# Sliding-window attention and an MLP on one core: another order for batch 3's exponentials, and one crossbar transposition ahead of six loads

## The chip, the core and the metric

The kernel runs on one core of a Trainium2 chip. A core has five engines, each with an instruction queue of its own that is worked off in order: TensorE (matrix products and transpositions, PE in the profile, with PEld for its weight loads), VectorE (DVE), ScalarE (ACT), GpSimd (POOL) and SyncE (SP), which in this kernel issues nearly all DMAs. They meet only through semaphores: an instruction that needs another engine's result waits at the head of its queue, and everything behind it waits too.

The metric is the device time of one execution in microseconds (us). The kernel before took 301.85 us, the median of three runs from 301.53 to 302.24.

## The reference

Eight batches, eight heads, 576 positions, 64 columns a head. Attention looks back over a window of 64 positions; the result, with heads side by side (512 columns), goes through a layer norm and a two-layer MLP with 2048 hidden units, and is added to itself:

```python
scores = scale * np.matmul(q, k.transpose(0, 1, 3, 2))
mask = (rel >= 0) & (rel < window)            # rel = query position - key position, window = 64
attn = softmax(np.where(mask, scores, -1e9))
x = np.matmul(attn, v)                        # then [batch, seq, heads * 64]
xn = (x - mu) / np.sqrt(var + 1e-06) * g_ln
out = x + np.maximum(xn @ w_ch1, 0.0) @ w_ch2
```

## The kernel before

**Groups and blocks.** The first 512 positions of a batch make a group (groups 0 to 7); the last 64 positions of all batches make group 8, the "tails", two batches to a block. A group has four blocks of 128 rows, written (group, block): (3,2) is the third block of batch 3.

**Attention of a block.** `s_pe` makes the scores on TensorE, the even heads in one PSUM bank and the odd ones in another ("par" 0 and 1, the two halves of a block). `s_exp` takes the exponential of one half on ScalarE (line 359), into the tile `pt`. `s_mask` multiplies both halves by the window's mask on VectorE (L369). `b_pe` multiplies by v on TensorE (L396, tile `xps`); `b_rows` divides by the row sums and takes mean and variance on VectorE (L416 to L429). `z_step` makes the norm's factors on GpSimd (tile `rsz`, L448 to L450) and, from group 3 on, the normalised rows z (L454); for group 2 `z_act` does the rows on ScalarE (L460). `zt_step` transposes z into `zT`, which layer 1 reads: on SyncE by a crossbar DMA (L474), or for the last block of groups 2, 3 and 5 on TensorE into the tile `ztp` (L478) with a copy by ScalarE (L481).

**Where the score tiles live.** PSUM is full, so scores borrow banks. For batch 3: (3,0) and (3,2) use the two "sc" banks, (3,1) the "xps" banks, which `b_pe` of (3,0) uses next, and (3,3) the banks "t0" and "t1", which the transpositions on TensorE use next, the `ztp` of (2,3) first among them.

**The MLP of a group** is a list of units. Group 2 has 30. Units 0 to 15 are layer 1 (`l1_half`, L642): eight matmuls into one of two PSUM buffers ("mm", used in turn), and a relu by ScalarE (L647) that frees the buffer. Units 0 to 7 read the first 256 rows of `zT`, units 8 to 15 the other 256. Units 16 to 29 are layer 2 in seven products (L575), whose results VectorE adds to x (L584, L588), and then SyncE stores. From group 3 on a layer-1 unit reads all 512 rows (L501).

**The order is written out by hand.** While the MLP of group g runs, the attention of batch g+1 is put between its units: `at(i, f, ...)` puts a call behind unit i, in slot i. Each engine gets its instructions in the order in which the calls are made, so a slot says at once where a call stands in the queue of every engine that it uses. The change moves entries of slots of g == 1 (slot 29) and g == 2.

**SyncE's queue in g == 2**, in the order of the slots: stores of the group before; `load_qk` and `load_v` of batch 4 (slots 0 and 3); `load_tail` of tail block 0, six loads, q, k and v of two batches (slot 4, L104 to L106); `zt_step` of (3,0) (slot 8); the two crossbar transpositions of batch 4's q (slot 13, L265); `zt_step` of (3,1) and (3,2) (slots 14 and 18); then copies of v (L201, L203), stores, and the loads of the next batch. `cast_tail` (GpSimd, L115 to L118) reads the tail loads in slot 24.

**GpSimd in g == 2**: the factors and rows z of the blocks, `after_mask` (L362), a one-element copy that reads the last masked tile and so holds GpSimd's casts of batch 4 (L154) until VectorE has finished the masks, the casts of v (L182) and the tails. z has three buffers, so z(3,3) takes the one of z(3,0) once its transposition has read it.

Of the kernel before, what the change touches and what calls it, by code (L numbers as in the profile page):

```python
# [18 lines left out]
def kernel(  # L19
# [927 lines left out]
    for g in range(NGRP):  # L947
# [7 lines left out]
        def at(i, f, *a):  # L955
            slots[min(i, len(slots) - 1)].append((f, a))
# [56 lines left out]
        if g == 1:  # L1013
            at(0, cast_qk, 2, 0, (0,))
            at(0, after_mask, 1, 3)
            at(0, cast_qk, 2, 0, (1,))
            at(0, cast_qk, 2, 1, (0,))
            at(0, alloc_v, 2)
            at(0, alloc_qkT, 2)
            at(1, t_main, 2, 0, 0)  # L1020
            at(1, b_pe, 1, 2, "t")
            at(1, b_pe, 1, 3, "sc")
            at(1, b_rows, 1, 2)
            at(1, z_step, 1, 2)
            at(1, b_rows, 1, 3)
            at(1, z_step, 1, 3)
            at(1, cast_qk, 2, 1, (1,))
            at(2, z_dve, 1, 2)
            at(3, t_main, 2, 1, 0)
            at(4, t_main, 2, 0, 1)  # L1030
            at(4, z_dve, 1, 3)
            for c in (0, 2):
                at(4, cast_v, 2, c, c + 2)
                at(5, part_vB, 2, c)
            at(5, zt_step, 1, 2)
            at(7, zt_step, 1, 3, "dve")
            at(10, t_main, 2, 1, 1)
            for n, i in enumerate((3, 2, 4)):
                at(8, w2_sums, i, 4, 8)
            at(7, s_pe, 2, 0)  # L1040
            at(7, s_pe, 2, 1, False, "xps")
            at(8, s_exp, 2, 0, 0, 1)
            at(9, s_mask, 2, 0)
            at(9, w2_sums, 1, 0, 8)
            at(10, s_exp, 2, 1, 0)
            at(11, s_exp, 2, 1, 1)
            at(12, s_sums, 0, 4, 1, 2)
            at(12, s_mask, 2, 1)
            at(16, s_sums, 4, 8, 1, 2)
            at(20, s_sums, 0, 8, 3)  # L1050
            at(22, s_sums, 0, 8, 4)
            for j in range(4):
                i = (13, 16, 22, 22)[j]
                at(i, b_pe, 2, j, "sc" if j == 3 else "xps")
                if j < 2:
                    at(i, s_mm, 2, j + 2)
                    at(19, s_mask, 2, j + 2)
                i = (13, 17, 25, 25)[j]
                at(i, b_mult, 2, j)
                if j == 3:  # L1060
                    i = 30
                at(i, b_stats, 2, j)
                at(i, z_step, 2, j)
                if j < 3:
                    at((17, 20, 26)[j], z_act, 2, j)
                    at((17, 20, 26)[j], zt_step, 2, j)
            at(6, load_qk, 3, 0)
            at(8, load_qk, 3, 1)
            at(10, load_v, 3, 0, 4)
            at(8, alloc_qkT, 3)  # L1070
            at(8, cast_qk, 3, 0)
            at(14, cast_qk, 3, 1, (0,))
            at(17, cast_qk, 3, 1, (1,))
            at(18, alloc_v, 3)
            at(18, cast_v, 3, 0, 2)
            at(18, cast_v, 3, 2, 4)
            at(21, part_vB, 3, 0, 4)
            at(29, s_pe, 3, 0)
            at(29, s_pe, 3, 1, False, "xps")
            at(29, s_exp, 3, 0, 0, 1)  # L1080
            for i, (x, half) in zip((12, 21, 18, 24), ((0, 0), (1, 0), (0, 1), (1, 1))):
                at(i, t_main, 3, x, half, 0)
        if g == 2:
            at(0, load_qk, 4, 0)
            at(0, load_qk, 4, 1)
            at(0, s_exp, 3, 1, 0)
            at(0, s_mask, 3, 0)
            at(1, s_exp, 3, 1, 1)
            at(2, s_mask, 3, 1)
            at(3, load_v, 4, 0, 4)  # L1090
            at(3, b_pe, 3, 0)
            at(3, s_pe, 3, 2)
            at(3, s_pe, 3, 3, False, "t")
            at(6, zt_step, 2, 3, "act")
            for i, x in enumerate(((2, 0), (2, 1), (3, 0), (3, 1))):
                at(3 + i, s_exp, 3, *x)
            at(4, z_act, 2, 3)
            at(5, s_mask, 3, 2)
            at(5, b_rows, 3, 0)
            at(5, z_step, 3, 0)  # L1100
            at(7, s_mask, 3, 3)
            at(7, alloc_qkT, 4)
            at(7, after_mask, 3, 3)
            at(7, cast_qk, 4, 0)
            at(7, cast_qk, 4, 1)
            for j in range(1, 4):
                at(9, b_pe, 3, j, ("xps", "t", "sc")[j - 1])
                at((9, 10, 12)[j - 1], b_rows, 3, j)
                at((9, 10, 12)[j - 1], z_step, 3, j)
            for j, i in enumerate((8, 14, 18, 25)):  # L1110
                at(i, zt_step, 3, j)
        elif g > 1 and b < B:
            tail = TAILS.get(g)
            at(2, b_pe, b, 0)
            at(2, b_rows, b, 0)
            at(2, z_step, b, 0)
            at(2, s_pe, b, 2)
            at(2, s_exp, b, 2, 0, 1)
            at(3, s_mask, b, 2)
            if tail:  # L1120
                r, i = NGRP - 1, tail[0]
                at(2, s_pe, r, i, False, "t")
                at(4, s_exp, r, i, 0)
                at(5, s_exp, r, i, 1)
                at(5, s_mask, r, i)
                at(7, b_pe, b, 1)
                at(7, b_pe, r, i, "t")
                at(7, s_mm, b, 3)
                at(7, b_rows, b, 1)
                at(7, z_step, b, 1)  # L1130
                at(8, s_mask, b, 3)
                at(8, b_rows, r, i)
                at(9, z_step, r, i)
                at(12, b_pe, b, 2)
                at(12, b_pe, b, 3, "sc")
                at(16, zt_step, r, i)
            else:
                at(2, s_pe, b, 3, False, "t")
                at(4, s_exp, b, 3, 0)
                at(5, s_exp, b, 3, 1)  # L1140
                at(5, s_mask, b, 3)
                at(7, b_pe, b, 1)
                at(7, b_pe, b, 2, "t")
                at(7, b_pe, b, 3, "sc")
                at(7, b_rows, b, 1)
                at(7, z_step, b, 1)
            if g + 2 < B:
                at(5, alloc_qkT, g + 2)
                at(5, after_mask, *((NGRP - 1, tail[0]) if tail else (b, 3)))
                at(5, cast_qk, g + 2, 0)  # L1150
                at(5, cast_qk, g + 2, 1, (0,))
                at(11, cast_qk, g + 2, 1, (1,))
            for j, i in ((2, 12), (3, 19)):
                at(i, b_rows, b, j)
                at(i, z_step, b, j)
            for j in range(4):
                at((2, 14, 18, {3: 25, 5: 25}.get(b, 23))[j], zt_step, b, j)
# [31 lines left out]
                at((15, 15, 20, 22)[i - 1], s_sums, 6, 8, i)  # L1189
        for n, i in enumerate(TAILS.get(g + 1, ())):  # L1190
            if n == 0:
                at(4, load_tail, i)
                at(24 if i < 2 else 18, cast_tail, i)
                at(27 if i < 2 else 22, t_tail, i, 0)
                at(29 if i < 2 else 22, t_tail, i, 1)
            else:
                at(25, load_tail, i)
# [48 lines left out]
```

## Time and profile before

| what | before |
|---|---|
| median of three runs | 301.85 us (301.53 to 302.24) |
| the profiled execution | 301.72 us, clock of TensorE 0.996 |
| its span, first to last instruction | 300.0 us |
| TensorE busy | 290.4 us, 97% |
| VectorE, GpSimd, ScalarE busy | 219.3, 164.9, 154.4 us |
| a relu, L647 | 0.60 us |
| an exponential of a half, L359 | 0.60 us |
| a layer-1 matmul of 256 columns, L642 | 0.27 us, pipelined |

A line of the timeline gives the start and the length in us, the engine, the line of the kernel, the operation, output and inputs, their shapes and how many were merged; brackets at its end hold the time that the engine sat idle before it and who ended that. A line of the waits gives who waited for whom: us in total, times, longest. Instructions of one engine overlap in the pipeline, so that one starts 0.48 us behind the last although each takes 0.60. The DMA issues of SyncE (SPq) give the time of issuing, not of the transfer; how long a transfer takes to land is told by tile, as minimum, median and maximum.

Of the stretch that the change touches: unit 0 of group 2 starts at 87.70 us, the first unit of group 3 at 121.05.

### The profile page before, as it was taken

What the parts mean: (1) busy time and instruction counts of PE and PEld (TensorE: products, weight loads), DVE (VectorE), ACT (ScalarE), POOL (GpSimd) and SP (SyncE); (2) the same over time, 40 slices, a digit from 0 to 9 for tenths busy, and PEclk for the clock granted to TensorE, in tenths of its full rate; (3) what the DMA queues carried; (4) which work ended last, traced back from release to release, by engine and by line L of the source; (5) the groups of instructions that cost most, each with busy time, mean ns of one, the idle gap of its engine ahead of it and who ended that gap; (6) DMA issues with size and microseconds to landing.
All of it is one profiled execution on the core that took longest, in us unless ns stands there. A gap on an engine that the chain in (4) does not pass through costs nothing.

```text
span 300.0 us, 7816 instructions
## 1 busy us (share of the span) xinstructions
PE 290.4 (97%) x3183; PEld 206.2 (69%) x3183; DVE 219.3 (73%) x414; ACT 154.4 (51%) x260; POOL 164.9 (55%) x243
## 2 busy tenths in 40 slices
PE   7889999999998999999999999999999999999993
PEld 3657545888887888547854786469646854788883
DVE  2771398899984794679757866699568785789982
ACT  4576647587348624874177428842574056306500
POOL 4688886765741986289608960788038407024300
PEclk9999999999999999999999999999999999999998
DMA  7999999979968999999299998991729498003014
GB/s 188 260 379 341 385 287 286 237 227 301 181 132 272 265 189 167 252 291 164 51 266 305 188 176 263 298 162 39 219 46 184 69 174 199 20 17 142 1 37 105
DMA packets 113765, 58.22 MB, mean 194 GB/s; under 512 B 83137, under 2 KB 104705, under 8 KB 113730
## 3 DMA queue, kind: packets, MB, share of 16 engines
q1 hardware_dynamic: 113296, 57.34, 79.1%
q8 instruction: 25, 0.41, 0.6%
q10 hardware_dynamic: 434, 0.40, 0.4%
q14 instruction: 10, 0.08, 0.1%
HBM read 38.80 MB, written 9.44 MB: 161 GB/s over the span
## 4 chain that ended last, share of the span: by engine, by line
PE 85%; DMA 4%; SPq 4%; POOL 2%; issue 1%; ACT 1%; DVE 1%; POOLq 0%; ACTq 0%
PE hps L501 26%; PE pA L575 12%; PE hph L642 10%; PE pB L575 9%; PE pC L575 8%; PE xps L396 4%; PE ch L659 4%; PE sc L349 3%; DMA w1s<-in_moe_w_ch_dram 3%; PE lA L698 2%; PE tp L276 2%; SPq L176 2%; DMA zT<-z 1%; SPq L87 1%; PE lC L698 1%
## 5 line engine op out<-in xcount | busy, mean ns | idle before, releaser
L501 PE MATMUL hps<-zT,w1g 128*128 128x512 f16 x352 | 80.2, 379 | 0.0
L505 ACT ACTIVATE hrT<-hps 128x512 f16<-128x512 f32 x88 | 52.8, 600 | 36.8 <-PE hps L501 33.7
L501 PEld LDWEIGHTS <-w1g 128*128 128x128 f16 x352 | 33.1, 98 | 38.0 <-issue 1.8
L575 PEld LDWEIGHTS <-sS 128*128 128x128 f16 x512 | 49.4, 98 | 5.7
L359 ACT ACTIVATE pt<-sc 128x512 f16<-128x512 f32 x72 | 39.7, 601 | 19.6 <-PE sc L349 18.9
L448 POOL TENSOR_SCALAR rsz<-mvg 128x1 f32<-128x1 f32 x32 | 10.5, 328 | 64.3 <-DVE mvg L429 54.6
L575 PEld LDWEIGHTS <-hrT 128*128 128x128 f16 x384 | 36.7, 98 | 6.9 <-ACT hrT L505 0.8
L369 DVE TENSOR_TENSOR pt<-pt,mask 128x1024 f16<-128x1024 f16 x32 | 24.6, 775 | 20.1 <-ACT pt L359 20.1
L642 PE MATMUL hph<-zT,w1g 128*128 128x256 f16 x320 | 38.1, 273 | 0.3 <-ACT hrT L647 0.2
L154 POOL CAST qk<-qk 128x1024 f16<-128x1024 f32 x29 | 33.0, 1157 | 8.2 <-DMA qk<-in_q_dram 6.6
L642 PEld LDWEIGHTS <-w1g 128*128 128x128 f16 x320 | 30.4, 98 | 5.0 <-issue 0.4
L575 PE MATMUL pC<-w2s,sS 128*128 128x256 f16 x256 | 30.9, 273 | 0.0
L575 PE MATMUL pA<-wT,sS 128*128 128x256 f16 x256 | 30.9, 273 | 0.0
L647 ACT ACTIVATE hrT<-hph 128x512 f16<-128x512 f32 x40 | 23.9, 601 | 11.4 <-PE hph L642 11.1
L257 ACT COPY qkT<-tp 128x1024 f16<-128x1024 f16 (+1 forms) x18 | 17.3, 963 | 23.1 <-PE tp L276 22.1
L549 DVE TENSOR_TENSOR sS<-hrT 128x1024 f16<-128x1024 f16 (+2 forms) x41 | 27.3, 665 | 1.8 <-ACT hrT L505 1.8
L420 DVE TENSOR_TENSOR xn<-xps,rcp 128x256 f32<-128x256 f32 (+1 forms) x50 | 25.8, 539 | 1.5 <-DMA out_dram<-xn 0.8
L426 DVE BATCH_NORM_STATS2 stats<-xn 128x6 f32<-128x512 f32 x36 | 25.0, 695 | 1.2
L454 POOL TENSOR_SCALAR z<-xn,rsz 128x512 f16<-128x512 f32 x24 | 22.3, 928 | 5.2 <-DMA zT<-z 2.8
L449 POOL TENSOR_TENSOR rsz<-rsz,mhalf 128x1 f32<-128x1 f32 x32 | 21.0, 658 | 2.7
L182 POOL CAST vA<-v 128x1024 f16<-128x1024 f32 (+1 forms) x18 | 17.1, 964 | 4.2 <-DMA v<-in_v_dram 4.0
L396 PEld LDWEIGHTS <-pt 128*64 128x64 f16 x576 | 11.6, 110 | 9.6 <-issue 5.1
(120 smaller groups left out, 418.8 us busy)
## 6 DMA issues: line engine op xcount, KB each, us to landing
qk<-in_q_dram SPq DMA_DIRECT2D x16, 512.0 KB, 6.1
qk<-in_k_dram SPq DMA_DIRECT2D x16, 512.0 KB, 6.7
out_dram<-xn SPq DMA_DIRECT2D x32, 256.0 KB, 3.1
v<-in_v_dram SPq DMA_DIRECT2D x28, 256.0 KB, 7.1
w2s<-in_moe_w_ch_dram SPq DMA_DIRECT2D x9, 512.0 KB, 8.4
w1s<-in_moe_w_ch_dram SPq DMA_DIRECT2D x4, 512.0 KB, 7.4
tk<-in_k_dram SPq DMA_DIRECT2D x8, 256.0 KB, 4.5
tv<-in_v_dram SPq DMA_DIRECT2D x8, 256.0 KB, 5.1
```

Source lines behind the costliest of these rows:

```text
L154: nc.gpsimd.tensor_copy(out=dst[:, :].rearrange("p (a j) e d -> p a e j d", j=j), in_=t[:, :].rearrange("p (a e j d) -> p a e j d", e=2, j ...
L359: nc.scalar.activation(out=o, in_=i, func=AF.Exp, bias=0.0, scale=scale)
L369: nc.vector.tensor_tensor(out=ptv, in0=ptv, in1=mb, op=ALU.mult)
L396: nc.tensor.matmul(out=tiles[h // n][64 * r:64 * r + 64, h % n, :D + 1], lhsT=pt[:, par, hp, r, :], rhs=rhs, start=True, stop=True)
L420: nc.vector.tensor_tensor(out=xn[:, n * i:n * i + n], in0=xps[:, :, 0:D], in1=rcp_b, op=ALU.mult)
L426: nc.vector.bn_stats(out=stats, in_=xv)
L501: nc.tensor.matmul(out=hps, lhsT=w1g[:, kc, 128 * hc:128 * (hc + 1)], rhs=zT[g][:, kc, :], start=(kc == 0), stop=(kc == NKC - 1),)
L505: nc.scalar.activation(out=hrT[:, hc, :], in_=hps, func=AF.Relu, bias=0.0, scale=1.0)
L549: nc.vector.tensor_tensor(out=o, in0=x, in1=y, op=op)
L575: nc.tensor.matmul(out=o, lhsT=a[:, c, 128 * p:128 * p + 128], rhs=wv[:, c, :], start=(first and (p == 0 or split_c) and c == 0), stop=(c ...
L642: nc.tensor.matmul(out=hps[:, e], lhsT=w1g[:, kc, 128 * hc:128 * (hc + 1)], rhs=zT[g][:, kc, 256 * half:256 * half + 256], start=(kc == 0) ...
L647: nc.scalar.activation(out=hrT[:, 2 * i:2 * i + 2, 256 * half:256 * half + 256], in_=hps, func=AF.Relu, bias=0.0, scale=1.0)
```

## The change

Three things. The second half of (3,0)'s exponentials goes from slot 29 of g == 1 to slot 0 of g == 2, and the halves of (3,1) from slots 0 and 1 to slots 1 and 2. The exponentials of (3,3) come ahead of those of (3,2), and the masks likewise; `after_mask` follows the mask that is now the last. And in g == 2 the six tail loads go from slot 4 to slot 9, behind the crossbar transposition of z(3,0) in slot 8; in other groups they stay in slot 4.

```diff
         if g == 1:
...
-            at(29, s_exp, 3, 0, 0, 1)
+            at(29, s_exp, 3, 0, 0)
...
         if g == 2:
             at(0, load_qk, 4, 0)
             at(0, load_qk, 4, 1)
-            at(0, s_exp, 3, 1, 0)
+            at(0, s_exp, 3, 0, 1)
             at(0, s_mask, 3, 0)
-            at(1, s_exp, 3, 1, 1)
+            at(1, s_exp, 3, 1, 0)
+            at(2, s_exp, 3, 1, 1)
             at(2, s_mask, 3, 1)
             at(3, load_v, 4, 0, 4)
             at(3, b_pe, 3, 0)
             at(3, s_pe, 3, 2)
             at(3, s_pe, 3, 3, False, "t")
             at(6, zt_step, 2, 3, "act")
-            for i, x in enumerate(((2, 0), (2, 1), (3, 0), (3, 1))):
+            for i, x in enumerate(((3, 0), (3, 1), (2, 0), (2, 1))):
                 at(3 + i, s_exp, 3, *x)
             at(4, z_act, 2, 3)
-            at(5, s_mask, 3, 2)
+            at(5, s_mask, 3, 3)
             at(5, b_rows, 3, 0)
             at(5, z_step, 3, 0)
-            at(7, s_mask, 3, 3)
+            at(7, s_mask, 3, 2)
             at(7, alloc_qkT, 4)
-            at(7, after_mask, 3, 3)
+            at(7, after_mask, 3, 2)
...
         for n, i in enumerate(TAILS.get(g + 1, ())):
             if n == 0:
-                at(4, load_tail, i)
+                at(9 if g == 2 else 4, load_tail, i)
```

## The prediction

> **What bounds the kernel now.** I read, in this order, the page's busy times, TensorE's waits, TensorE's timeline around the change, then ScalarE, GpSimd and SyncE in the same stretch.
>
> ```profile
> PE 290.4 (97%) x3183; PEld 206.2 (69%) x3183; DVE 219.3 (73%) x414; ACT 154.4 (51%) x260; POOL 164.9 (55%) x243
> ```
>
> TensorE is the bound, so the change can only win what TensorE idles. All of its waits from 85 to 121 us, the stretch that the change touches (the same view from 121 us to the end is empty: afterwards TensorE never waits, so a gain or a loss at 121 us goes through to the end one to one):
>
> ```profile
> PE ztp L478 <- ACT pt L359: 1.1, 1, 1.1
> PE ztp L478 <- POOL z L454: 0.3, 1, 0.3
> PE hph L642 <- ACT hrT L647: 0.2, 1, 0.2
> ```
>
> Their places in TensorE's timeline; the last column is idle time and who ended it:
>
> ```profile
> 89.85 2.01 PE L642 MATMUL hph<-zT,w1g 128*128 128x256 f16 x16 [0.23 <-ACT hrT L647]
> ...
> 96.64 0.38 PE L478 MATMUL ztp<-ident,z 128*128 128x128 f16 x4 [1.10 <-ACT pt L359]
> ...
> 115.94 0.40 PE L478 MATMUL ztp<-ident,z 128*128 128x128 f16 x4 [0.25 <-POOL z L454]
> ```
>
> Matmuls are pipelined, so I count in start times. Eight matmuls of a unit take 0.87 us (1.75 for 16, as 83.53 to 85.28 shows). Unit 2 could have started at 87.70 + 1.75 = 89.45 and started at 89.85: 0.40 lost. The ztp at 96.64 could have started at 92.74 + 24 x 0.109 = 95.36: 1.28 lost. The one at 115.94 could have at 113.78 + 1.75 = 115.53: 0.41 lost.
>
> ScalarE, where the first two waits end (L359 exponentials, L647 relus, L460 and L481 the normalised rows z(2,3) and the copy of their transpose):
>
> ```profile
> 93.83 0.60 ACT L647 ACTIVATE hrT<-hph 128x512 f16<-128x512 f32 x1 [0.62 <-PE hph L642]
> 94.32 0.59 ACT L359 ACTIVATE pt<-sc 128x512 f16<-128x512 f32 x1
> 94.80 0.81 ACT L460 ACTIVATE z<-xn,rsz 128x512 f16<-128x512 f32 x1
> 95.51 0.59 ACT L647 ACTIVATE hrT<-hph 128x512 f16<-128x512 f32 x1
> 95.98 0.60 ACT L359 ACTIVATE pt<-sc 128x512 f16<-128x512 f32 x1
> 96.46 0.61 ACT L647 ACTIVATE hrT<-hph 128x512 f16<-128x512 f32 x1
> 97.06 0.59 ACT L481 COPY zT<-ztp 128x512 f16<-128x512 f16 x1
> 97.54 0.60 ACT L359 ACTIVATE pt<-sc 128x512 f16<-128x512 f32 x1
> 98.03 0.60 ACT L647 ACTIVATE hrT<-hph 128x512 f16<-128x512 f32 x1
> ```
>
> The reader is to see that no row from 94.32 to 98.03 has an idle time behind it: ScalarE works without a pause while TensorE waits 1.10. One starts every 0.48 us (0.71 behind z). GpSimd and SyncE, where the third wait comes from:
>
> ```profile
> 115.12 0.77 POOL L454 TENSOR_SCALAR z<-xn,rsz 128x512 f16<-128x512 f32 x1 [2.79 <-DMA zT<-z]
> ```
> ```profile
> 94.79 8.68 SPq L176 DMA_DIRECT2D v<-in_v_dram  x4
> 103.51 1.03 SPq L104 DMA_DIRECT2D tq<-in_q_dram  x1
> 104.59 0.64 SPq L105 DMA_DIRECT2D tk<-in_k_dram  x1
> 105.27 1.09 SPq L106 DMA_DIRECT2D tv<-in_v_dram  x1
> 106.41 1.45 SPq L104 DMA_DIRECT2D tq<-in_q_dram  x1
> 107.91 1.64 SPq L105 DMA_DIRECT2D tk<-in_k_dram  x1
> 109.58 1.01 SPq L106 DMA_DIRECT2D tv<-in_v_dram  x1
> 110.71 1.69 SPq L474 DMA_TRANSPOSE zT<-z  x1
> ```
>
> z(3,3) has three buffers to rotate through and takes the one of z(3,0); z(3,0) is written by 99.88, but its transposition is issued only at 110.71, behind v and the six tail loads.
>
> **Part 1: the exponentials.** Eight remain, at the same 0.48 us; TensorE's order does not change. Worked forward with these rows, a relu starting 0.22 behind the last matmul start slot of its unit (unit ends 101.42, relu 101.64), and TensorE 0.05 behind a release (relu ended 89.80, unit 2 started 89.85). exp(3,0,0) 88.25; relu 0, which waits for unit 0 (87.70 + 0.87 + 0.22), 88.79; exp(3,0,1) 89.27; relu 1 89.75; exp(3,1,0) 90.23; relu 2 90.71; exp(3,1,1) 91.19, done 91.79. Unit 2 then starts at 89.45, so the 0.40 goes. But b_pe(3,0) writes into the "xps" banks that held the scores (3,1), and those are free only at 91.79: it starts at 91.85, where it started at 91.79 before. The stall has moved and become 0.06 longer.
>
> From there: scores until 92.80; unit 4; relu 4 at 92.80 + 0.87 + 0.22 = 93.89 (93.83 before). exp(3,3,0) fits before it, in ScalarE's pause of 0.62. Behind relu 4 the same list runs as in the rows above, only with (3,3,1) first and (3,2,0), (3,2,1) later: z 94.86, relu 5 95.57, exp 96.04, relu 6 96.52, copy 97.00, exp 97.48, relu 7 97.96, done 98.56. The wait of the ztp does go: the (3,3) scores sat in the banks it needs, their exponentials now end at 94.98, and it starts behind z at 95.73. But unit 9 reuses the PSUM buffer of unit 7 and needs relu 7: 98.61, against 98.03 + 0.60 + 0.05 = 98.68 before. Units 7 and 8 wait for relus 5 and 6 and for the copy (97.59), which unit 8, the first on rows 256 to 511, reads. Of 1.28 us TensorE keeps 0.07. The release of "xps" I take for the whole tile; if it goes by bank, half of b_pe(3,0)'s 32 matmuls (0.38 us) run before the wait and the gain is 0.2 more.
>
> What else moves is covered. DVE masks (3,3) first and (3,2) last, at about 98.2 to 98.8; b_pe(3,2) comes at 100. The mask of (3,0) ends at 90.6 instead of 90.2, needed at 91.85. The mark that GpSimd takes from the last mask (L362) still stands behind z(3,0), which ends at 99.88, so the casts of batch 4 don't move. If these covers went, mask (3,2) would have to be 1.2 us late first.
>
> **Part 2: the transposition.** On SyncE zt(3,0) passes six loads; those, the two q transpositions of batch 4 and zt(3,1), zt(3,2) keep their order. z(3,0) is ready, so SyncE does not wait. Issued at 103.5 and landing in 4.2 us (that of 110.71), or 9.3 at worst (the longest of v's), it frees the buffer at 107.8 to 112.8; z(3,3) can run when its factors are there (110.98 + 1.35 = 112.33) and must be done by 115.46. So the 0.41 goes entirely. The six loads end later by 1.2 to 1.7, the transposition's issue time. Their casts start at 117.85 and the last load landed near 109.58 + 4.7 = 114.3, so 1.7 later is hidden; GpSimd reaches them earlier, at 115.1.
>
> [...]
>
> What is late next: the first layer-1 unit of the next group, at 121.05, reads all of zT(3). zt(3,2) is issued at 116.53 and lands 4.4 us later:
>
> ```profile
> L474 SPq DMA_TRANSPOSE zT<-z x1: 1226/1226/1226, 116.5 to 116.5; - x1
> ...
> DMA to landing us min/median/max: 4.4/4.4/4.4
> ```
>
> That is 120.92, 0.13 us ahead of its reader, which now comes at 120.57. This is the tightest place of the change. SyncE's whole list up to there is the same, so from the same rows zt(3,2) would land when it did (gain cut to 0.08); but the 1.69 of the transposition is now issued while queued loads still drain, and loads that are held up (1.45, 1.64, against 0.64 for the same kind) take less when started later, so I expect SyncE 0 to 1 us earlier at 116.5, and take 0.5. Then nothing is lost.
>
> **Sum.** 0.07 + 0.41 = 0.48 us off. The profiled execution took 301.72 (span 300.0 and 1.72 around it); 301.24 from it. The median of the three times is 0.13 above it: 301.85 - 0.48 = 301.4.
>
> **Rivals.** (a) The landing of zT(3,2) does not move, and TensorE waits at 120.97: -0.08, 301.8. For it: the order and total of SyncE's queue are unchanged; against: the slack argument above. (b) Waits of TensorE vanish and nothing takes their place: 0.40 + 1.28 + 0.41 = 2.1 off, 299.8. For it: TensorE's list of waits taken alone; against: ScalarE's unbroken row of starts. (c) "xps" goes by bank: 0.2 more, 301.2; no row tells. (d) Slower: the tail loads behind the transposition all go at the price of the slower three (1.45 + 1.64 + 1.01 = 4.1 against 2.76 for the first three), 1.35 more on SyncE; zT(3,2) lands at 122.27, the unit starts at 122.32, 1.27 later than before: 303.1. It decides from the point where zt(3,2) is issued 0.1 us later than 116.53. For it: the queue is backed up; against: all those bytes were in the queue before too.
>
> **How the numbers follow.** The forecast has 0.50; (a) 0.17, (b) 0.10, (c) 0.12, (d) 0.11. A change of 0.2% (0.6 us) is about what a measurement of this kernel can tell from none; the three times before lie within 0.71. -0.48 is close to that bound, so the forecast gives 0.19 to faster and 0.31 to the same; (a) goes to the same but for 0.02, (b) to faster, (c) 0.07 and 0.05, (d) nearly all to slower. Together 0.37, 0.51, 0.12. The range leaves (b) and (d) out: 300.8, (c) with half the spread of the times, to 302.2, (a) with the same. The forecast's own range is 301.0 to 301.8.
>
> **What would show it.** Right: TensorE idles before b_pe(3,0) at about 91.8 (a wait on ScalarE's exponential), the ztp starts near 95.7 and TensorE is held up again by L647 between 96 and 98.6; unit 9 starts within 0.2 of 98.6; no wait of GpSimd for a DMA before z(3,3); the ztp behind 113.7 follows without a gap. Wrong: the 1.28 stays gone to 99 us, or the unit at 121 waits for a DMA on zT, or the scores (4,0) near 117.5 for the q transpositions, which landed at 117.1 before.

## The result: 301.31 us, 0.26% less, and the profile after

| | before | after |
|---|---|---|
| median, 20 executions each | 302.25 us (301.23 to 303.18) | 301.31 us (300.67 to 302.49) |
| ratio of the means | | 0.9974, 95% interval 0.9962 to 0.9987 |
| profiled execution | 301.72 us, span 300.0 | 301.25 us, span 299.5 |

The forecast was 301.4 and 0.48 us off; the interval is 0.4 to 1.15 us off. The size fits. That 301.4 itself is met so closely is luck: the kernel before came out at 302.25 here, where the forecast started from 301.85, and with the larger gain this cancels. One execution of the kernel `all_three` below ran at a granted clock of 0.755 throughout and took 371.85 us; its time is left out and its profile is not used.

What the profile shows does not fit: in this execution the stretch that the change touches won next to nothing. (Where a kernel has added lines, the line numbers behind them are a few higher.) TensorE's waits from 85 to 122.5 us in the changed kernel (us in total, times, longest):

```profile
PE xps L396 <- ACT pt L359: 0.4, 1, 0.4
PE hph L642 <- ACT zT L481: 0.4, 1, 0.4
PE hps L501 <- DMA zT<-z: 0.3, 1, 0.3
```

All three waits of before are gone, and three others stand in their places. In TensorE's timeline of the changed kernel:

```profile
92.80 2.79 PE L642 MATMUL hph<-zT,w1g 128*128 128x256 f16 x24
95.72 0.40 PE L478 MATMUL ztp<-ident,z 128*128 128x128 f16 x4
96.20 1.03 PE L642 MATMUL hph<-zT,w1g 128*128 128x256 f16 x8
97.65 2.02 PE L642 MATMUL hph<-zT,w1g 128*128 128x256 f16 x16 [0.41 <-ACT zT L481]
...
113.73 1.91 PE L575 MATMUL pC<-w2s,sS 128*128 128x256 f16 x16
115.48 0.39 PE L478 MATMUL ztp<-ident,z 128*128 128x128 f16 x4
...
121.02 1.25 PE L501 MATMUL hps<-zT,w1g 128*128 128x512 f16 x5 [0.31 <-DMA zT<-z]
```

The ztp at 95.72 starts 0.82 us earlier against unit 0 than before. But unit 8, two rows on, starts at 97.65, behind a wait for the copy of that ztp: 10.05 us behind unit 0, where it was at 10.04; the ztp of (3,3) follows at 115.48 without a gap (113.73 + 1.75); and the first unit of group 3 starts at 121.02, where it started at 121.05 before (33.42 us behind unit 0 after, 33.35 before). ScalarE shows the first half of this:

```profile
88.75 0.60 ACT L647 ACTIVATE hrT<-hph 128x512 f16<-128x512 f32 x1
89.24 0.59 ACT L359 ACTIVATE pt<-sc 128x512 f16<-128x512 f32 x1
...
91.15 0.65 ACT L359 ACTIVATE pt<-sc 128x512 f16<-128x512 f32 x1
...
94.85 0.81 ACT L460 ACTIVATE z<-xn,rsz 128x512 f16<-128x512 f32 x1
...
97.94 1.38 ACT L647 ACTIVATE hrT<-hph 128x512 f16<-128x512 f32 x2
```

Relu 0 starts 1.15 us behind unit 0 and not 1.50, but exp(3,1,1), which frees the xps banks, starts only at 91.15, and relu 7 at 97.94, 10.34 us behind unit 0, where it was at 10.33. SyncE and GpSimd show the second half; the line under SyncE's is that of the two q transpositions in the kernel before:

```profile
103.81 1.62 SPq L474 DMA_TRANSPOSE zT<-z  x1
105.47 0.71 SPq L104 DMA_DIRECT2D tq<-in_q_dram  x1
106.22 0.62 SPq L105 DMA_DIRECT2D tk<-in_k_dram  x1
106.90 0.58 SPq L106 DMA_DIRECT2D tv<-in_v_dram  x1
107.52 2.02 SPq L104 DMA_DIRECT2D tq<-in_q_dram  x1
109.58 0.75 SPq L105 DMA_DIRECT2D tk<-in_k_dram  x1
110.38 1.16 SPq L106 DMA_DIRECT2D tv<-in_v_dram  x1
111.64 3.85 SPq L265 DMA_TRANSPOSE qkT<-qk  x2
115.59 2.54 SPq L474 DMA_TRANSPOSE zT<-z  x2
```
```profile
112.51 2.60 SPq L265 DMA_TRANSPOSE qkT<-qk  x2
```
```profile
112.69 0.76 POOL L454 TENSOR_SCALAR z<-xn,rsz 128x512 f16<-128x512 f32 x1
```

z(3,3) has no wait for a DMA any more and comes 2.4 us earlier. The six tail loads take 6.06 us to issue, 1.0 less than before, but the two q transpositions behind them 3.85 instead of 2.60. So zt(3,2) is issued at 116.91, no earlier than before (116.53), lands 4.1 us later at 120.97, and TensorE stands waiting.

For the other kernels I give times from the start of unit 0 of group 2, since the start of that unit, which lies ahead of everything that the change touches, differs by up to 0.7 us between executions (from about 87.5 us in the second profile of the changed kernel to about 88.2 in `exps_only`). "Wait" is in start times, as in the prediction. "Three profiles" are three profiled executions of the same kernel.

| kernel | b_pe(3,0) | unit 9 | wait for z(3,3) | wait for zT(3,2) | group 3's first unit |
|---|---|---|---|---|---|
| before, three profiles | 4.09, 4.08, 4.09 | 10.99, 10.98, 10.98 | 0.42, 0.62, 0.53 | none | 33.35, 33.51, 33.52 |
| after, three profiles | 4.24, 4.24, 4.24 | 11.04, 11.03, 11.04 | none | 0.47, 0, 0.65 | 33.42, 32.95, 33.60 |
| exps_only | 4.24 | 11.04 | 0.93 | none | 33.88 |
| xbar_only | 4.09 | 10.98 | none | 0.64 | 33.54 |
| tail_v_late | 4.24 | 11.04 | none | none | 32.95 |
| tail_v_last | 4.24 | 11.04 | none | none | 32.94 |
| xps_free_early | 3.75 | 10.55 | none | 0.35 | 32.93 |
| z_on_dve | 4.25 | 10.36 | none | 0.80 | 33.58 |
| best | 3.76 | 9.87 | none | none | 31.78 |

### The profile page after: what moved, and what is told of

Read it like the earlier page. It is cut to its first block, busy times and chain, and to the rows that moved or that the text cites. A ratio compares the mean times of both kernels' runs of the same rounds, so it can differ in the third digit from the quotient of the medians.

```text
span 299.5 us, 7818 instructions
## 1 busy us (share of the span) xinstructions
PE 291.2 (97%) x3183; PEld 206.6 (69%) x3183; DVE 219.9 (73%) x414; ACT 154.1 (51%) x260; POOL 163.3 (55%) x243
## 4 chain that ended last, share of the span: by engine, by line
PE 84%; DMA 6%; SPq 2%; DVE 2%; ACT 2%; POOL 2%; issue 1%; POOLq 0%
PE hps L501 26%; PE pA L575 12%; PE pB L575 8%; PE pC L575 8%; PE hph L642 7%; PE xps L396 4%; PE ch L659 4%; PE sc L349 3%; DMA qk<-in_k_dram 3%; PE tp L276 3%; PE lA L698 2%; PE warm L869 2%; DMA tk<-in_k_dram 2%; DMA zT<-z 1%; PE lC L698 1%
## 5 line engine op out<-in xcount | busy, mean ns | idle before, releaser
L154 POOL CAST qk<-qk 128x1024 f16<-128x1024 f32 x29 | 32.4, 1132 | 9.1 <-PE sc L349 5.9
L647 ACT ACTIVATE hrT<-hph 128x512 f16<-128x512 f32 x40 | 24.0, 603 | 10.9 <-PE hph L642 10.6
L549 DVE TENSOR_TENSOR sS<-hrT 128x1024 f16<-128x1024 f16 (+2 forms) x41 | 26.3, 641 | 2.1 <-ACT hrT L505 2.0
```

The costliest lines, as they stand in the source:

```text
L154: nc.gpsimd.tensor_copy(out=dst[:, :].rearrange("p (a j) e d -> p a e j d", j=j), in_=t[:, :].rearrange("p (a e j d) -> p a e j d", e=2, j ...
L549: nc.vector.tensor_tensor(out=o, in0=x, in1=y, op=op)
L647: nc.scalar.activation(out=hrT[:, 2 * i:2 * i + 2, 256 * half:256 * half + 256], in_=hps, func=AF.Relu, bias=0.0, scale=1.0)
```

## The experiments

My theory at this point: ScalarE's order and the xps banks take back what part 1 freed; part 2 frees 0.4 us or more, and the landing of zT(3,2) takes it back in some executions. The rivals: the 0.8 us of the timing come from part 1, or from timed executions in which zT(3,2) is always in time.

### The kernel before, twice more

No edit.

> The kernel before, unchanged: what two equal kernels differ by, and a second profile. Both theories: ratio 1.000 within 0.002. The first theory (what the profile shows is what the timing measures) expects the same places as in the first profile to within 0.1 us: the ztp of (2,3) 8.9 us behind unit 0 of group 2, the first unit of group 3 33.35 us behind it, zT(3,2) landing about 0.1 us ahead of that unit. The second theory (zT(3,2) lands at times that differ from execution to execution) expects this landing to differ by more than 0.3 us from the first profile.

> The kernel before, a third look. My theory: unit 9 at 10.99 us behind unit 0, the wait for z(3,3) 0.4 to 0.9 us in start times, set by when the transposition of z(3,0) lands, and the first unit of group 3 at 33.35 to 33.85 us behind unit 0.

Ratio 0.9995 (0.9974 to 1.0015): equal kernels agree. The places repeat to 0.01 us up to unit 9. Behind that they do not: in the second profile zT(3,2) landed 2.3 us behind its issue instead of 4.4, and z(3,3) was waited for longer:

```profile
PE ztp L478 <- POOL z L454: 0.5, 1, 0.5
```

The wait that part 2 removes was 0.42 us in the execution that I predicted from, and 0.62 and 0.53 in the others.

### Each part alone

`exps_only` is the changed kernel with `at(4, load_tail, i)` as before:

```diff
-                at(9 if g == 2 else 4, load_tail, i)
+                at(4, load_tail, i)
```

> The exponentials' new order alone; the tail loads stay in slot 4. My theory, that ScalarE's order of work and the xps banks take back what the ztp's wait gave: TensorE idles ahead of b_pe(3,0) until 4.2 us behind unit 0, unit 9 starts 11.0 us behind unit 0 (before 10.99), and the wait for z(3,3) of 0.41 us stays: 0.0 to 0.1 us off, ratio 1.000. The rival, that the gain of the whole change (0.8 us by the timing) comes from here: ratio 0.9975.

Ratio 1.0002 (0.9987 to 1.0017). TensorE's waits in it:

```profile
PE ztp L478 <- POOL z L454: 0.8, 1, 0.8
PE xps L396 <- ACT pt L359: 0.4, 1, 0.4
PE hph L642 <- ACT zT L481: 0.4, 1, 0.4
```

The 1.1 us at the ztp of (2,3) and the 0.2 at unit 2 have become two waits of 0.4 and some that are too short for this view; unit 9 comes 0.06 us later than before, not 0.07 earlier. The timing shows no gain of part 1 alone, to within 0.5 us either way.

`xbar_only` is the kernel before with this line of the change alone:

```diff
-                at(4, load_tail, i)
+                at(9 if g == 2 else 4, load_tail, i)
```

> The six tail loads behind the transposition of z(3,0) alone; the exponentials as before. My theory: the ztp of (2,3) waits 1.1 us as before, the wait for z(3,3) is gone, and the first unit of group 3 waits for zT(3,2) by 0.3 to 0.5 us in the profile; by the timing 0 to 0.4 us off, ratio 0.9987 to 1.000. The rival, that in the timed executions zT(3,2) is in time and this part carries the gain: 0.4 us or more off, ratio 0.9987 or below.

Ratio 0.9992 (0.9977 to 1.0006), which holds both theories' values. Its waits:

```profile
PE ztp L478 <- ACT pt L359: 1.1, 1, 1.1
PE hps L501 <- DMA zT<-z: 0.5, 1, 0.5
PE hph L642 <- ACT hrT L647: 0.2, 1, 0.2
```

The wait for z(3,3) went and the one for zT(3,2) came; in this execution the second is the dearer.

### The changed kernel, twice more

No edit.

> The changed kernel, unchanged: a second profile and a second timing of it. My theory, that in it the first unit of group 3 starts when zT(3,2) lands, while in the kernel before TensorE waits for z(3,3) by 0.4 to 0.9 us: b_pe(3,0) again 4.24 us and unit 9 again 11.04 us behind unit 0 of group 2, the first unit of group 3 at 33.0 (nothing to wait for) to 33.5 us behind it, and 0.1 to 0.7 us off by the timing, ratio 0.9977 to 0.9997. The rival, that the first timing (0.9974) was all of it the change: 0.997 to 0.998 again.

> The changed kernel, a third look. My theory: b_pe(3,0) at 4.24 and unit 9 at 11.04 us behind unit 0, no wait for z(3,3), and the first unit of group 3 at 32.95 us or, where zT(3,2) lands later than that, at its landing, up to 33.5.

Ratio 0.998 (0.9966 to 0.9993): again faster than before. In the second profile zT(3,2) landed at 32.90 and group 3 did not wait, 0.4 to 0.57 us better than the three profiles of before; in the third it landed at 33.55, and TensorE lost more than the whole gain (the one line of its waits that the second does not have):

```profile
PE hps L501 <- DMA zT<-z: 0.5, 1, 0.5
```

So part 2's gain is there in one profiled execution in three.

### Taking the wait for zT(3,2) away

`tail_v_late` takes the two tail loads of v out of the six and issues them behind zt(3,2):

```diff
+                if g == 2:
+                    at(19, load_tail_v, i)   # the two loads of tv
```

> The changed kernel with the two tail loads of v issued behind the transposition of z(3,2), so that this is issued 1.7 us (0.57 and 1.15, the two issues) earlier. My theory, that the landing of zT(3,2) bounds the first unit of group 3: the unit starts at the end of the transpositions before it, 0.47 us earlier against unit 0 of group 2 than in the changed kernel (32.95 in place of 33.42 us), and the kernel takes 0.4 to 0.5 us less than the changed one: ratio to the kernel before 0.9955 to 0.9965. The rival, that the landing is late in the profile only: the same as the changed kernel, 0.997 to 0.998.

The first unit of group 3 starts at 32.95 to the digit. But the ratio is 0.9985 (0.9971 to 1.0), no better than the changed kernel: the copies into vB now stand behind those loads, and TensorE meets them 3.3 us later (TensorE's waits from 121 us on):

```profile
PE xps L401 <- DMA vB<-vA: 0.5, 1, 0.5
PE pB L580 <- DVE xn L593: 0.3, 1, 0.3
```

`tail_v_last` issues them behind the copies into vB, with their cast.

```diff
-                    at(19, load_tail_v, i)
+                    at(26, tail_v, i)        # the two loads of tv and the cast into vt
```

> The changed kernel with the two tail loads of v, and their cast, in slot 26 behind the copies into vB, so that neither zT(3,2) nor vB stands behind them. My theory: the first unit of group 3 at 32.95 us behind unit 0 of group 2 and no wait of TensorE for a DMA behind it; 0.47 us less than the changed kernel, 0.997 or below against the kernel before. The rival, that TensorE meets another late landing one step on (vB, or the v of the tails at its b_pe): the unit at 32.95, but the end no earlier than the changed kernel's, 0.998 to 0.999.

The unit is at 32.94, and vB is in time. The rival was right, one step further on than it said: ratio 0.9997 (0.9983 to 1.0011). The loads now hold up the stores of group 2, whose buffers VectorE needs for the rows of batch 4:

```profile
123.75 0.21 DVE L423 RECIPROCAL rcp<-xps 128x8 f32<-128x8 f32 x1 [2.17 <-PE xps L403]
125.46 0.69 DVE L427 TENSOR_TENSOR xn<-xps,rcp 128x512 f32<-128x512 f32 x1 [1.50 <-DMA out_dram<-xn]
```

By 129.22 VectorE has made this up: it is where it is in the changed kernel's second profile (129.12, with unit 0 of group 2 0.12 us earlier). GpSimd, which needs VectorE's mean and variance, has not. Its casts of batch 5 start at 130.01 and not at 129.02, and the second of them now starts just ahead of a mask:

```profile
130.99 1.04 POOL L161 CAST qk<-qk 128x1024 f16<-128x1024 f32 x1
```
```profile
131.02 1.55 DVE L376 TENSOR_TENSOR pt<-pt,mask 128x1024 f16<-128x1024 f16 x1
```

The mask took 0.77 us in the changed kernel's second profile. From here VectorE stays behind by about 0.8 us, until TensorE waits 0.6 us for it at 142. The same meeting stands in `tail_v_late` (cast at 131.33, mask at 131.70, 1.21 us) and, at another mask, in `best` below. Both kernels show that the landing of zT(3,2) did hold group 3's start, and that neither of the two places tried for the two loads is free.

### What ScalarE's row holds

`xps_free_early` puts one half one slot earlier:

```diff
-            at(2, s_exp, 3, 1, 1)
+            at(1, s_exp, 3, 1, 1)
```

> The changed kernel with the second half of (3,1) in slot 1, ahead of relu 2, so that the xps banks are free one ScalarE instruction (0.48 us) earlier. My theory, that their release by exp(3,1,1) sets b_pe(3,0) and ScalarE's chain behind it: b_pe(3,0) 3.77 us behind unit 0 (4.24 before), unit 9 10.58 (11.04), and the first unit of group 3 no earlier than the landing of zT(3,2), so that the 0.46 us is lost there: 33.0 to 33.5 us, ratio as the changed kernel's within 0.001. The rival, that TensorE's chain behind b_pe is set by something else: unit 9 stays at 11.0.

b_pe(3,0) at 3.75 and unit 9 at 10.55, both within 0.03 of what was expected. The waits from 85 us on:

```profile
PE hph L642 <- ACT zT L481: 0.4, 1, 0.4
PE hps L501 <- DMA zT<-z: 0.2, 1, 0.2
```

Of the 0.49 us that unit 9 gains, group 3's start keeps only as much as the landing of zT(3,2) allows: it starts 0.05 us behind that landing. Ratio 0.9981 (0.9964 to 0.9998), the changed kernel's within its uncertainty.

`z_on_dve` takes z(2,3) from ScalarE:

```diff
-            at(4, z_act, 2, 3)
+            at(4, z_dve, 2, 3)
```

> The changed kernel with z(2,3) made by VectorE, one look. My theory, that ScalarE's unbroken row sets unit 9: 0.71 us out of that row, unit 9 at 10.3 us behind unit 0 (11.04), b_pe(3,0) still at 4.24, and the first unit of group 3 no earlier than zT(3,2) lands, 32.9 to 33.5 us. The rival, that the transposition chain (z, ztp, copy) sets units 7 to 9: unit 9 moves by 0.3 us or less, since VectorE's z is not the last of that chain.

Unit 9 at 10.36: 0.68 of the 0.71 us. ScalarE's row set it, not the chain of z, ztp and copy: the ztp itself came only 0.29 us earlier. And all of it was lost again, on the landings in the first and third line:

```profile
PE hps L501 <- DMA zT<-z: 0.6, 1, 0.6
PE xps L396 <- ACT pt L359: 0.4, 1, 0.4
PE sc L349 <- DMA qkT<-qk: 0.3, 1, 0.3
PE hph L642 <- ACT zT L481: 0.3, 1, 0.3
```

### Together

`all_three` is `tail_v_last` with the last two edits.

```diff
-            at(2, s_exp, 3, 1, 1)
+            at(1, s_exp, 3, 1, 1)
-            at(4, z_act, 2, 3)
+            at(4, z_dve, 2, 3)
```

> The changed kernel with three more edits: the tail loads of v last, exp(3,1,1) in slot 1, and z(2,3) made by VectorE, which takes 0.71 us out of ScalarE's unbroken row. My theory, that ScalarE's row bounds units 7 to 9 and the landings bound group 3's start: unit 9 at 9.85 us behind unit 0 (11.04 less 0.46 less 0.73), the first unit of group 3 at 31.8 us, 1.6 us less than the changed kernel, ratio to the kernel before 0.991 to 0.994. The rival, that the landings do not move and hold TensorE: unit 9 at 9.85, but the first unit of group 3 at 32.9 or later, ratio 0.996 to 0.998.

Ratio 0.9948 (0.9929 to 0.9966), the lowest of the study: 300.25 us, the median of six executions. Without a profile to compare, where its 1.6 us lie is not shown.

`best` has the two edits as well, but issues the loads of v behind the stores of group 2 and casts them in slot 3 of group 3.

```diff
-                    at(26, tail_v, i)
+            if g == 2:
+                at(40, tail_v, 0)        # the loads alone, ahead of load_qk of batch 5
...
+        if g == 3:
+            at(3, tail_v_cast, 0)
```

> The changed kernel with exp(3,1,1) in slot 1, z(2,3) on VectorE, and the two tail loads of v behind the stores of group 2 (their cast in slot 3 of group 3). My theory, that ScalarE's row, then the landing of zT(3,2), then the stores behind the tail loads are the three things that hold TensorE: unit 9 at 9.85 us behind unit 0 of group 2 (changed kernel 11.04), the first unit of group 3 at 31.8 us (33.0 to 33.4), no wait of TensorE for a DMA and none of VectorE for a store, 1.2 to 1.7 us less than the changed kernel, ratio to the kernel before 0.992 to 0.994. The rival, that the loads of batch 5, now 1.2 us later, make a wait in group 3: the first unit of group 3 at 31.8 us, but 0.995 or above.

Unit 9 at 9.87 and group 3's first unit at 31.78, as expected, and none of the waits of before; ratio 0.9968 (0.9958 to 0.9977), an interval that overlaps that of `all_three`. It should have been 0.992 to 0.994. From group 3's first unit to the last matmul's end it takes 174.97 us, 0.81 more than the changed kernel, and neither theory had named why. GpSimd's and VectorE's timelines in it, and TensorE's waits from 85 us on:

```profile
127.36 1.04 POOL L114 CAST vt<-tv 128x1024 f16<-128x1024 f32 x1
129.01 0.19 POOL L371 COPY masked<-pt 128x1 f16<-128x1 f16 x1 [0.61 <-DVE pt L378]
```
```profile
127.44 1.50 DVE L378 TENSOR_TENSOR pt<-pt,mask 128x1024 f16<-128x1024 f16 x1 [1.94 <-ACT pt L368]
```
```profile
PE xps L405 <- DVE pt L378: 0.6, 1, 0.6
PE hph L651 <- ACT zT L490: 0.3, 1, 0.3
```

The mask of the tails, 0.69 us elsewhere, took 1.50, with GpSimd's cast started 0.08 us ahead of it; TensorE's b_pe of the tails waited. The tie is close. Five masks here start while such a cast runs: the three long ones of `tail_v_late`, `tail_v_last` and `best`, and two in the first two profiles of the changed kernel that took 0.67 and 0.77 us, where the cast was nearer its end. All five end 0.54 or 0.55 us behind the end of that cast. No run moved the cast alone, so that the cast is the cause is argued, not shown. If it is, the two engines meet here in another way than through semaphores, which the section on the core calls the only one: each of the five masks had already started. Whether a cast 1 us later brings the rest was not tried.

## Why the prediction was right or wrong

**Part 1** was right in its mechanism, and mis-sized by 0.13 us: unit 9 at 10.91 us behind unit 0 expected, 11.04 measured, which turns 0.07 us won into 0.05 lost. Half of it is relu 0, which starts 1.15 us behind unit 0 and not 1.09; with it all that follows in ScalarE's row moves. The second wait on ScalarE in the profile is for the copy (L481, at unit 8), which the prediction had too; relu 7 (L647), which it expected to see there, adds only 0.11 us at unit 9, too short for the list. b_pe(3,0) has 16 matmuls, not 32, which changes no sum. It waits for the whole of "xps", so rival (c) is out: TensorE's 0.44 us of idle time lies ahead of the first of its matmuls, not between the halves. Rival (b), waits that vanish with nothing in their place, is out by `exps_only`.

**Part 2**: the wait for z(3,3) went, as predicted. It was larger in other executions than the 0.41 that I read off one.

**The step that failed** is the one that I called the tightest: "I expect SyncE 0 to 1 us earlier at 116.5, and take 0.5. Then nothing is lost." Against unit 0, zt(3,2) was issued at 28.84, 29.05 and 29.01 us before and at 29.31, 29.05 and 29.29 after: 0.25 later in the mean, and not 0.5 earlier (0.15 of it stood already ahead of the loads). The loads did take 1.0 us less to issue. But the first q transposition, which now comes directly behind the six loads, as zt(3,0) did before, took 2.5 us instead of 1.24 and gave it back. This holds in every profile: 2.1 to 2.9 us in the nine with zt(3,0) ahead of the loads, 1.24 in the four without. So rival (a), to which I gave 0.17, is what two of three profiled executions show.

**The sum** came out right all the same, and partly by accident. Means over three profiled executions each, in us:

| piece of the span | before | after | difference |
|---|---|---|---|
| to unit 0 of group 2 | 87.86 | 87.68 | -0.18 |
| from there to group 3's first unit | 33.46 | 33.32 | -0.14 |
| from there to the last matmul's end | 174.23 | 174.16 | -0.07 |
| from there to the last instruction | 4.70 | 4.35 | -0.35 |
| span | 300.26 | 299.51 | -0.74 |

The total agrees with the two timings (0.79 and 0.60 us by the ratios). The first piece lies ahead of everything that the change touches; its values scatter over 0.3 us in the one kernel and 0.5 in the other. The third goes with part 1, by an effect that the prediction does not have: `exps_only` has 174.16, `xbar_only` 174.24. The last is not in the prediction either; it is told below. What the change does to its own stretch is between 0.25 us lost and 0.57 won, 0.14 won in the mean of these six, where 0.48 was forecast.

How much the landing of zT(3,2) costs in executions without the profiler stays open: the timings of `xbar_only` and of the changed kernel are compatible with 0 and with 0.5 us.

What counted on SyncE was the time to issue, and it was not the same for the same 128 KB: 1.62 us for zt(3,0), 0.71 and 2.02 for the two tail loads of q behind it. Against unit 0, the issue of the six loads ended 1.0 us later than before in the first profile of each kernel, and not 1.2 to 1.7.

## What to carry to other kernels

A stall of the bounding engine is worth the slack up to the next thing it meets and no more: here the 1.3 us ahead of a transposition was worth nothing, because the engine that ended it was itself without a pause. Add up the work of that engine over the stretch first, and shorten it (0.68 of 0.71 us reached unit 9) or reorder it around the one release that matters (0.49 where 0.46 was expected). Here, moving one transfer ahead of six moved the long issue to what then stood behind them (2.1 to 2.9 us for the first q transposition, where it was 1.24); look at the landing of every transfer with as little in hand as zT(3,2) has here, 0.13 us, in more than one execution, before counting a gain: in three executions of the changed kernel that landing came at 33.37, 32.90 and 33.55 us behind unit 0.

## What the runs showed of the hardware

**A fetch of instructions beside a transfer.** The trace has 25 packets of 16 KB on a queue that the profile calls instruction. TensorE has 6366 matmuls and weight loads, about 255 for each packet, and VectorE, the next, has 414 by the same count, so I take them for fetches of TensorE's: an estimate from these counts, which no run shows directly. Those near 119 us took 0.88 to 1.42 us. Where such a fetch starts 1.8 to 2.2 us behind the issue of zt(3,2), the transposition lands 3.9 to 4.4 us behind it, and where it starts later, 2.3:

| kernel | fetch behind issue, us | landing behind issue, us |
|---|---|---|
| before, three profiles | 2.04, 2.29, 1.90 | 4.38, 2.33, 4.37 |
| after, three profiles | 1.78, 1.80, 1.82 | 4.06, 3.85, 4.26 |
| exps_only, xbar_only, xps_free_early, z_on_dve | 2.05, 2.14, 1.83, 2.17 | 4.18, 4.17, 3.86, 4.18 |
| tail_v_late, tail_v_last, best | 3.95, 5.41, 4.54 | 2.34, 2.33, 2.33 |

In the first profile of before, 15 of the 16 parts of the transfer had reported by 118.86 us and the last one at 120.92. There is no exception in 13 executions. The tie is closer than the table says: in all nine late ones the last part comes 1.05 to 1.11 us behind the end of the fetch, though that end lies anywhere from 2.74 to 3.32 us behind the issue. But no run moved the fetch alone, so that the fetch is the cause is argued, not shown. If it is, issuing this transposition a little earlier does not make it land earlier by as much: it lands with the fetch, or, issued some 2.3 us ahead of the fetch, about 2 us sooner. The two answers for zT(3,2) side by side, the changed kernel and then `best`:

```profile
DMA to landing us min/median/max: 4.1/4.1/4.1
```
```profile
DMA to landing us min/median/max: 2.3/2.3/2.3
```

**The end of the program.** From the last matmul's end to the last instruction it takes 4.70, 4.70 and 4.71 us in the kernel before and 4.35, 4.34 and 4.36 after, with the same stores landing 3.0 and 3.3 us behind that matmul in both. Most of the difference lies between two semaphore instructions of GpSimd at the very end: they start 0.37 us apart in the first profile of before and 0.08 in that of after, 0.29 of the 0.35. Other kernels have 4.35 (`xps_free_early`, `z_on_dve`, `best`: 4.36), 4.55 (`xbar_only`, `tail_v_late`, `tail_v_last`, within 0.01) or 4.83 (`exps_only`). The instructions there are the same in before and after; why they take longer in some programs was not tried. This also bears on the two parts alone: their ratios add up to a gain of 0.0006, where the whole change gained 0.0020 and 0.0026, and 0.31 us (0.0010) of the gap, if the executions without the profiler have it too, is that this piece fell by 0.17 us in `xbar_only`, rose by 0.13 in `exps_only` and fell by 0.35 with both. It is 0.35 us of a difference of 0.7 in the profiles, and it lies more than 170 us behind the exponentials and transfers that were moved: at this size a timing alone does not tell what a change did.
